# A transformer block on one core: side sums in an idle chain, Q's products and denominators reordered, result adds deferred

## The chip, the core and the metric

The kernel runs on one core of one Trainium2 chip. The core has a matmul engine (PE, TensorE), a vector engine (DVE), an activation engine (ACT), GpSimd (POOL) and a sync engine (SP) that, like POOL, issues DMAs here. The metric is the device time of one execution in microseconds (us), lower is better. A profiled execution gives a trace with every engine's instructions.

## The reference

The input x is 2048 rows of 512 in f32. A vector c gives six modulation rows through `silu(c) @ w_mod`. What is computed:

```python
h = layernorm(x) * (1 + ca) + sa
q, k, v = split(h @ wqkv)                      # 32 heads of 16
pq, pk = phi(q), phi(k)                        # phi(t) = where(t > 0, t + 1, exp(t)) + 1e-6
kv = einsum("bhsd,bhse->bhde", pk, v);  z = einsum("bhsd->bhd", pk)
o = einsum("bhqd,bhde->bhqe", pq, kv) / (einsum("bhqd,bhd->bhq", pq, z)[..., None] + 1e-6)
x = x + ga * (o @ wo)
h = layernorm(x) * (1 + cb) + sb
x = x + gb * (mish(h @ w1 + b1) @ w2)          # 512 -> 1792 -> 512
```

## The kernel before

**Tiling.** The 2048 rows are four blocks b of 512, each of four tiles t of 128 rows. Every f32 operand of a matmul is split into a rounded high part (a copy, usually on ACT) and the low part that is left (a subtraction, usually on DVE); `split` (L71) does that, with a `yield` between the two, and `mm3` (L65) multiplies with three matmuls: high x high, high x low, low x high. A unit of one 128-row tile is twelve matmuls.

**Stages, in PE's order.** For b = 1 to 3 (L726 to L775): four K units (`k_unit`), whose result goes through `phi` and `split`, then four `g_unit`s, which sum pk^T x xn over all rows into four banks gacc (so that kv = wv applied later, L930 to L944). Between them lie the transposes of the next block. In the last round come wq's splits, wo's scaling and the sums z. Then Q: for blocks 0 and 1 together by seven products instead of eight (`q_sevens` L339, one level of Strassen-Winograd, with sums of x in `q_right` and of wq in `q_left`), for blocks 2 and 3 by plain units (`q_unit`). `attend` (L778) makes the denominators on PE (den), their reciprocals on DVE, writes them to DRAM and reads them back spread over the heads (rd, by POOL's queue; for block 3 by SP's), and after `wait` more steps multiplies q with rd and splits it (qs). The matrices m = kv x wo (L954 to L957) are then used by `o_unit` (L821), which adds to the rows r. Blocks 0 to 3 are normalised again (`norm_sums` L828, `norm_each` L842, `norm_tile` L860) and transposed.

The second half, w1, Mish and w2, again uses seven products per pair of w1's columns. `rows` (L675) loads w1 and makes its sums, `columns` those of h, `product` (L1025) is one product of six matmuls (two halves c, three matmuls each). A pair is `pair_begin` (a11, a12), `pair_early` (s1, s2), `pair_middle` (s3), `pair_end` (a22, s4). Several products add up in one bank, with copies u1, u2, u3 of it taken by ACT between them; `add` (L1035) adds bank and copy on DVE, and `mish` or `later`/`mish_b` follow on ACT. `two_pairs` runs the first two pairs of a chunk interleaved. In the first chunk the gaps hold w2's product of block 0 (`d_unit`), in the last chunk (blocks 2 and 3) the units `e_unit` of a seven-product form of w2; its left operands come from `left_sums` (L1238), its right ones from `w2_sums` (L630).

**What sets the order.** The schedule is written out by hand: each engine runs its instructions in the order in which the program issues them. Beside the main line, side work is written as Python generators. `spawn` (L50) puts one into `fresh`; `tick` (L53) appends `fresh` to `running` and then takes one step of each generator in `running`, oldest first. So a tick, usually one per unit or product of PE, is what spreads side work. SBUF tiles come from one pool of 101 tiles of 512 columns (`sb`), PSUM banks from pools of 4 (acc), 3 (h) and 1 (tp); a new tile waits for the last reader of the one whose place it takes. SP and POOL issue their DMAs in order, too.

**Where the diff falls in the trace.** Early rows are `rows(0, 1)` and `rows(1, 1)` (L724). Before, the first starts with the last round's first K unit, the second is run to its end in one go after m (L958). `q_left` (L304) starts beside the g units of round 2, `q_right` (L313) beside rounds 1 and 2. In rounds 1 and 2, x's splits for tiles 2 and 3 start beside the g units of tiles 0 and 1 (L769). `W2_AT` (L628) says beside which unit of block 1's w2 stage a `w2_sums` starts; `SUMS_KEPT` names the two that stay in SBUF.

Of the kernel before, what the change touches and what calls it, by code (L numbers as in the profile page):

```python
# [13 lines left out]
P = 128  # L14
# [11 lines left out]
def block_kernel(ctx: ExitStack, tc: tile.TileContext, x, wqkv, wo, w1, b1t, w2, c, wmodt, out):  # L26
# [21 lines left out]
    running, fresh = [], []  # L48
# [195 lines left out]
    def phi(p, name, dst):  # L244

        e, r = sb(f"e_{name}"), sb(f"relu_{name}")
        act.activation(e, p, AF.Exp)  # L247
        act.activation(r, p, AF.Relu)  # L248
        yield
        dve.scalar_tensor_tensor(dst, e, 1.0, r, op0=ALU.min, op1=ALU.add)  # L250
# [89 lines left out]
    def q_sevens(side):  # L340

        pa, pc, u1, u2, u3 = {}, {}, {}, {}, {}

        def result(b, g, p, u):
            if u is not None:
                c = sb(f"cq_{b}_{g}")
                dve.tensor_tensor(c, p, u, op=ALU.add)
                p = c
            pq[b, g] = sb(f"q_{b}_{g}")
            spawn(phi(p, f"q_{b}_{g}", pq[b, g]))  # L350
# [277 lines left out]
    W2_AT = {0: 6, 1: 5, 2: 0, 3: 1, 6: 2, 10: 3, 12: 4}  # L628
# [97 lines left out]
    for b in range(1, NB):  # L726
# [3 lines left out]
        for t in range(4):  # L730
            k_unit(b, t)
            if b + 2 < NB:
                load_x(b + 2, t)
            if b == NB - 2:
                load_wqkv(0, t)
                if t == 1:
                    spawn(q_right(1))
            if last and t == 0:
                spawn(early_rows[0])
            if last:  # L740
                xn_split(b, t)
            elif t >= 2:
                xn_split(b, t - 2)
            tick()
# [4 lines left out]
        for t in range(4):  # L749
# [6 lines left out]
            if b == 1 and t == 1:  # L756
                spawn(q_right(0))
            if b == 2 and t < 2:
                spawn(q_left(t))
            if last:  # L760
                load_x(0, t, "r")
                for k in ((0, 1), (2,), (3,), ())[t]:
                    spawn(split(f"wq_{k}", wraw[0, k], wq, k))
                if t == 2:
                    z_unit()
                if t == 3:
                    spawn(z_side())
            elif t < 2:
                xn_split(b, t + 2)  # L769
# [58 lines left out]
    def norm_sums(b):  # L828

        sums = {}  # L830
        for n in range(6):
            if n < 4:
                sums[n] = act_sums("n", b, n, xt["r", b, n])
            if 0 < n < 5:
                sums_eps("n", b, n - 1, sums[n - 1])
            if n > 1:
                sums_shift("n", b, n - 2, sums[n - 2])
                v = xt["n", b, n - 2] = sb(f"n_{b}_{n - 2}")
                ln_apply("n", b, n - 2, xt["r", b, n - 2], v, act)
            yield  # L840
# [19 lines left out]
    def norm_tile(b, t):  # L860

        v = xt.pop(("r", b, t))
        if t % 2:
            ln_stats("n", b, t, v)
            ln_eps("n", b, t, t + 1)
            ln_rstd("n", b, t, t + 1)
            yield
            ln_apply("n", b, t, v, v, dve)
        else:
            sums = act_sums("n", b, t, v)  # L870
            yield
            sums_eps("n", b, t, sums)
            yield
            sums_shift("n", b, t, sums)
            ln_apply("n", b, t, v, v, act)
# [53 lines left out]
    next(early_rows[1])  # L929
# [7 lines left out]
    attending = attend(0, 4)  # L937
    next(attending)
    next(attending)
# [14 lines left out]
    for g in range(4):  # L954
        m_ps = ps("acc", f"m_ps_{g}")
        mm3(m_ps, [h[:, P * g:P * (g + 1)] for h in kvs[0]], wos[g], True, True)
        spawn(split(f"m_{g}", m_ps, ms, g))  # L957
# [80 lines left out]
    def pair_begin(c0, g, tags):  # L1038
# [3 lines left out]
        c11 = sb(f"c11_{g}")  # L1042
        add(c11, product(g, "a12", "b21", tags[1]), u1)
        return pa, c11

    def later(p, f, wait=0):
        for _ in range(wait):
            yield
        mish_b(p, f)
        yield  # L1050

    def pair_early(c0, g, pa, c11, tag):
# [5 lines left out]
        spawn(mish(c11, c0, 2 * g))  # L1060
        return pa, pc, u2

    def pair_middle(g, pa, pc, u2):
        u3, c22 = sb(f"u3_{g}"), sb(f"c22_{g}")
        product(g, "s3", "t3", onto=pa)
        act.activation(u3, pa, AF.Copy)  # L1066
        add(c22, pc, u3)
        spawn(later(c22, 2 * g + 1, 1))

    def pair_end(c0, g, pa, pc, u2, step=True):  # L1070
        c12 = sb(f"c12_{g}")
# [4 lines left out]
        add(c12, pc, u2)  # L1076
        spawn(later(c12, 2 * g, 1))
# [3 lines left out]
    def pair_unit(c0, g, odd, between):  # L1081
        begun = pair_begin(c0, g, ("tp" if odd else "h", "h"))
        tick()
        state = pair_early(c0, g, *begun, "h")
# [8 lines left out]
    def two_pairs(c0, g0, g1, begun, between):  # L1093

        s0 = pair_early(c0, g0, *begun[0], "h")
# [4 lines left out]
        pa, c11 = begun[1]  # L1100
# [3 lines left out]
        spawn(mish(c11, c0, 2 * g1))  # L1104
# [94 lines left out]
    banks, rq, U = {}, {}, {}  # L1199

# [27 lines left out]
    def left_sums(g):  # L1228
# [3 lines left out]
        dve.tensor_tensor(a22, a21, a22, op=ALU.add)  # L1232
        dve.tensor_tensor(a21, a11, a21, op=ALU.subtract)
        yield
        dve.tensor_tensor(a11, a22, a11, op=ALU.subtract)
        dve.tensor_tensor(a12, a12, a11, op=ALU.subtract)
# [4 lines left out]
    def left_trail(g):  # L1241
        yield
        yield
        yield from left_sums(g)
# [48 lines left out]
    for n, g in enumerate(pairs):  # L1293
# [97 lines left out]
```

## Time and profile before

| | |
|---|---|
| median of 3 runs | 516.07 us (515.71 to 516.18) |
| profiled execution | 515.32 us, span 513.6 us |
| PE busy | 493.6 us, 2640 matmuls, mean granted clock 0.993 |
| DVE, ACT, POOL busy | 368.9, 298.4, 144.5 us |
| HBM read, written | 62.92, 33.03 MB |

Times in the trace count from the span's start. A row of a timeline gives the start, the duration, the engine, the line, what is written and read, and in brackets the engine's idle time ahead with the instruction that ended it. A row of the waits gives who waited for whom: us in total, times, longest. A row of the windows gives the stretch, its length, the busy time of PE, of PE's weight loads, DVE, ACT and POOL with their counts, the clock granted to PE (1.00 is full), the DMA engines' mean busy share, and GB/s. Busy time of an engine is not its speed: a matmul is drawn with its whole way through the array, and the next may start before it ends.

### The profile page before, as it was taken

To read this page: it belongs to the slowest core of one execution; us is meant where nothing else is said; L and a number is where in the kernel's file an instruction comes from. 1 tells how busy PE (TensorE), PEld (TensorE's weight loads), DVE (VectorE), ACT (ScalarE), POOL (GpSimd) and SP (SyncE) were. 2 spreads that over 40 slices of the span, in tenths; PEclk is the share of its full clock that TensorE was granted. 3 is DMA by queue.
4 is the path that set the end of the run, shared out by engine and by line. 5 is a ranking of instruction groups with operands and counts; after the bars stand their busy time and mean duration, and the time that the engine had idled before them with its cause. 6 is when DMAs were issued, how large, how long until landed. Compare 5 with 4: busy or idle time off the path is not lost.

```text
span 513.6 us, 7722 instructions
## 1 busy us (share of the span) xinstructions
PE 493.6 (96%) x2640; PEld 413.5 (81%) x2640; DVE 368.9 (72%) x713; ACT 298.4 (58%) x535; POOL 144.5 (28%) x246
## 2 busy tenths in 40 slices
PE   8999997999998999998999999999998999999997
PEld 6788785878776877886788888888786888899997
DVE  6896889798979577965678763679953575549862
ACT  6868597655544498647777564358354544468200
POOL 3573020000031324111344310513454231345200
PEclk9999999999998998999999999999999999999999
DMA  8715445046844305517999956999997463497512
GB/s 298 277 39 127 123 102 144 21 133 208 260 131 123 76 18 187 199 67 265 325 340 358 333 177 210 260 373 321 378 358 219 119 185 82 125 237 214 144 42 83
DMA packets 66765, 98.58 MB, mean 192 GB/s; under 512 B 7405, under 2 KB 31861, under 8 KB 66726
## 3 DMA queue, kind: packets, MB, share of 16 engines
q0 software_dynamic: 29360, 45.31, 32.3%
q1 hardware_dynamic: 37220, 52.51, 30.6%
q8 instruction: 21, 0.34, 0.3%
q10 hardware_dynamic: 146, 0.26, 0.1%
q14 instruction: 18, 0.15, 0.1%
HBM read 62.92 MB, written 33.03 MB: 187 GB/s over the span
## 4 chain that ended last, share of the span: by engine, by line
PE 71%; DVE 11%; ACT 8%; issue 5%; DMA 3%; POOL 0%; ACTq 0%; POOLq 0%; DVEq 0%
PE p_a L1031 17%; PE p_s L1031 7%; PE oacc L69 5%; PE oacc L67 5%; PE oacc L68 5%; PE m L69 5%; PE m L68 5%; PE m L67 5%; PE o L67 2%; PE o L69 2%; PE o L68 2%; PE gacc L69 2%; PE gacc L68 2%; ACT x L201 1%; PE gacc L67 1%
## 5 line engine op out<-in xcount | busy, mean ns | idle before, releaser
L1036 DVE TENSOR_TENSOR c<-p_s,u 128x512 f32<-128x512 f32 x28 | 19.3, 691 | 72.0 <-ACT u L1066 61.5
L1059 ACT ACTIVATE u<-p_a 128x512 f32<-128x512 f32 x12 | 7.2, 598 | 30.6 <-PE p_a L1031 30.6
L1023 ACT ACTIVATE ub<-c,b1c 128x512 f32<-128x512 f32 x28 | 20.0, 717 | 3.7 <-DVE c L1036 3.5
L1291 POOL DMA_DIRECT2D wt_m<-w2t x20 | 14.0, 702 | 26.0 <-PE m L69 17.2
L891 ACT ACTIVATE hf_n<-tp_n,mc 128x512 f32<-128x512 f32 x16 | 11.7, 771 | 15.7 <-PE tp_n L889 15.7
L192 POOL TENSOR_TENSOR rs_n<-rs_n,half 128x1 f32<-128x1 f32 x16 | 10.0, 626 | 30.5 <-DVE rs_n L187 14.5
L790 POOL DMA_DIRECT2D rden_d<-rden x3 | 2.2, 717 | 54.0 <-DVE rden L788 54.0
L1041 ACT ACTIVATE u<-p_a 128x512 f32<-128x512 f32 x14 | 8.3, 594 | 15.0 <-PE p_a L1031 15.0
L247 ACT ACTIVATE e_k<-pk 128x512 f32<-128x512 f32 x16 | 9.5, 594 | 11.9 <-PE pk L69 11.9
L1066 ACT ACTIVATE u<-p_a 128x512 f32<-128x512 f32 x14 | 8.3, 594 | 13.0 <-PE p_a L1031 13.0
L673 POOL DMA_DIRECT2D w2b<-w2d x20 | 10.6, 552 | 18.1 <-issue 5.6
L250 DVE SCALAR_TENSOR_TENSOR ku<-e_k,relu_k 128x512 f32<-128x512 f32 x16 | 11.0, 689 | 6.4 <-ACT relu_k L248 6.4
L814 DVE TENSOR_TENSOR r<-o,r 128x512 f32<-128x512 f32 x16 | 11.0, 686 | 6.4 <-PE o L69 6.4
L1036 DVE TENSOR_TENSOR c<-p_a,u 128x512 f32<-128x512 f32 x14 | 9.6, 689 | 7.2 <-PE p_a L1031 5.0
L250 DVE SCALAR_TENSOR_TENSOR q<-e_q,relu_q 128x512 f32<-128x512 f32 x16 | 10.8, 689 | 5.1 <-ACT relu_q L248 5.1
L201 ACT ACTIVATE x<-x,nb_x,rs_x 128x512 f32<-128x512 f32 x15 | 11.4, 809 | 5.3 <-DVE nb_x L196 4.9
L192 POOL TENSOR_TENSOR rs_x<-rs_x,half 128x1 f32<-128x1 f32 (+1 forms) x10 | 7.4, 742 | 24.2 <-DVE rs_x L187 23.4
L1000 ACT ACTIVATE u<-p_a,b1c 128x512 f32<-128x512 f32 x14 | 9.5, 680 | 7.2 <-PE p_a L1031 7.2
L667 POOL DMA_DIRECT2D wb<-w2d x14 | 9.9, 709 | 12.7 <-ACT u L1000 8.4
L259 POOL DMA_DIRECT2D ku<-ku x8 | 7.1, 893 | 18.6 <-DVE ku L250 17.9
L878 POOL DMA_DIRECT2D nd<-r x8 | 4.5, 565 | 26.7 <-ACT r L201 26.7
L802 DVE SCALAR_TENSOR_TENSOR q<-q,rd 128x512 f32<-128x512 f32 x16 | 10.4, 690 | 1.7 <-DMA rd<-rden_d 1.7
(1569 smaller groups left out, 1986.1 us busy)
## 6 DMA issues: line engine op xcount, KB each, us to landing
wm<-in_wmodt_dram SPq DMA_DIRECT2D x24, 256.0 KB, 2.8
w2b<-w2d POOLq DMA_DIRECT2D x20, 256.0 KB, 6.2
wt_m<-w2t POOLq DMA_DIRECT2D x20, 256.0 KB, 3.6
r<-in_x_dram SPq DMA_DIRECT2D x16, 256.0 KB, 3.2
x<-in_x_dram SPq DMA_DIRECT2D x15, 256.0 KB, 4.8
w1p<-in_w_dram SPq DMA_DIRECT2D x14, 256.0 KB, 3.6
w2r<-in_w_dram SPq DMA_DIRECT2D x14, 256.0 KB, 3.5
wb<-w2d POOLq DMA_DIRECT2D x14, 256.0 KB, 4.4
```

Source lines behind the costliest of these rows:

```text
L67: pe.matmul(o, st[0], mv[0], start=start, stop=False)
L68: pe.matmul(o, st[0], mv[1], start=False, stop=False)
L69: pe.matmul(o, st[1], mv[0], start=False, stop=stop)
L192: pool.tensor_tensor(y, y, half[:, lo:hi], op=ALU.pow)
L201: act.activation(dst, t, AF.Identity, bias=nb[key, b][:, j:j + 1], scale=rs[key, b][:, j:j + 1])
L250: dve.scalar_tensor_tensor(dst, e, 1.0, r, op0=ALU.min, op1=ALU.add)
L814: dve.tensor_tensor(r, p, r, op=ALU.add)
L891: act.activation(hf[b, j], p, AF.Identity, bias=mc[:, 12 + j:13 + j], scale=mc[:, 16 + j:17 + j])
L1023: act.activation(u, p, AF.Mish, bias=b1c[:, f:f + 1])
L1031: pe.matmul(p, st, mv, start=onto is None and c == 0 and i == 0, stop=c == 1 and i == 2, skip_group_check=onto is not None)
L1036: dve.tensor_tensor(out, p, u, op=ALU.add)
L1291: pool.dma_start(v, w2t[g][:, :, SUM[name], :])
```

## The change

A second list of generators, `idle_work`, is stepped at the end of each tick, only its first two (three in the last chunk). Into it go Q's right and left sums, the early rows, the left sums of the last chunk and the two kept w2 sums; several of them start later than before. Splits of x in rounds 1 and 2 start beside the K units, as in round 3. In `q_sevens`, s1 comes after a22, and phi of a sum waits one tick. den(0) comes after the first Q unit of block 2, den(1) after the third, with m's products between. Block 0's norm starts tile by tile. The adds of the pairs' results become generators of their own, issued in the tick behind. One `norm_next` goes, `norm_tile` yields once more, and the order of the first units in the last chunk's gaps changes.

The diff, cut to its core:

```diff
+    def spawn_idle(gen):
+        idle_work.append(gen)
     def tick():
...
+        for g in idle_work[:width[0]]:          # width is [2], in the last chunk [3]
+            if next(g, "end") == "end":
+                idle_work.remove(g)
...
-    def phi(p, name, dst):
+    def phi(p, name, dst, wait=False):
+        if wait:
+            yield
...
         for o in range(2):                       # in q_sevens
-            pc[o] = q_product(o, "s1", "t1", ("h", "acc")[o])
             q_product(o, "s3", "t3", onto=pa[o])
             u3[o] = copy(pa[o], f"qu3_{o}")
-            result(1, 2 + o, pc[o], u3[o])
-            side(3 + o)
+        side(3)
         for o in range(2):
             result(0, 2 + o, q_product(o, "a22", "t4", onto=pa[o]), None)
+        side(4)
+        for o in range(2):
+            pc[o] = q_product(o, "s1", "t1", ("h", "acc")[o])
+            result(1, 2 + o, pc[o], u3[o])
         side(5)
...
-    W2_AT = {0: 6, 1: 5, 2: 0, 3: 1, 6: 2, 10: 3, 12: 4}
+    W2_AT = {0: 6, 1: 5, 2: 0, 3: 1, 6: 2}
...
                 if t == 1:                       # K units of rounds 1 to 3
-                    spawn(q_right(1))
-            if last and t == 0:
-                spawn(early_rows[0])
-            if last:
-                xn_split(b, t)
-            elif t >= 2:
-                xn_split(b, t - 2)
+                    spawn_idle(q_right(1))
+            if last and t < 2:
+                spawn_idle(q_left(t))
+            if last and t == 2:
+                spawn_idle(early_rows[0])
+            xn_split(b, t)
...
             if b == 1 and t == 1:                # g units
-                spawn(q_right(0))
-            if b == 2 and t < 2:
-                spawn(q_left(t))
+                spawn_idle(q_right(0))
...
-            elif t < 2:
-                xn_split(b, t + 2)
...
-    def norm_sums(b):
...
+    def norm_first(t):                           # one step each: nothing, sums, eps, shift, apply
...
             sums_shift("n", b, t, sums)          # norm_tile
+            yield
             ln_apply("n", b, t, v, v, act)
...
-    next(early_rows[1])
...
-    attending = attend(0, 4)                     # after kv's product
-    next(attending)
-    next(attending)
...
-    spawn(attending)
+    attending = attend(0, 3)
     for g in range(4):
         q_unit(2, g)
+        if g == 0:
+            next(attending)
+            next(attending)
         if g == 1:
+            spawn(attending)
+        if g == 2:
             spawn(attend(1, 4))
+        if g == 1:
             spawn(mod_side(range(12, 16), 1))
         load_x(3, g, "r")
+        if g == 2:
+            for k in range(4):                   # m's products, from behind this loop
...
         tick()
-    run(early_rows[1])
     for g in range(4):
         q_unit(3, g)
         tick()
         if g == 1:
             for t in range(4):
                 o_unit(0, t)
+                spawn(norm_first(t))
...
-            spawn(norm_sums(0))
+            spawn_idle(early_rows[1])
...
-        c11 = sb(f"c11_{g}")                     # pair_begin
-        add(c11, product(g, "a12", "b21", tags[1]), u1)
-        return pa, c11
+        c11, p = sb(f"c11_{g}"), product(g, "a12", "b21", tags[1])
+        def result():
+            add(c11, p, u1)
+            yield
+            yield from mish(c11, c0, 2 * g)
+        spawn(result())
+        return pa
+    def result_b(p, u, f):
+        c = sb(f"cb_{f}")
+        add(c, p, u)
+        yield
+        mish_b(c, f)
...
-        add(c22, pc, u3)                         # pair_middle
-        spawn(later(c22, 2 * g + 1, 1))
+        spawn(result_b(pc, u3, 2 * g + 1))
...
-        add(c12, pc, u2)                         # pair_end
-        spawn(later(c12, 2 * g, 1))
+        spawn(result_b(pc, u2, 2 * g))
...
-            norm_next()                          # first chunk, g == 1, ahead of two_pairs
...
+        for n, (d, u, v, op) in enumerate(...):  # left_sums: a step for each sum if fine
+            if fine or n == 2:
+                yield
+            dve.tensor_tensor(d, u, v, op=op)
...
+        if n in (3, 5):                          # last chunk
+            spawn_idle(w2_sums(SUMS_KEPT[n // 2 - 1]))
...
-            two_pairs(L, pairs[0], g, begun, (gap(0, 0), gap(1, 0)))
+            two_pairs(L, pairs[0], g, begun, (gap(0, 0), gap(0, 1)))
             for i in range(2):
-                spawn(left_trail(pairs[i]))
+                spawn_idle(left_trail(pairs[i]))
         else:
-            pair_unit(L, g, n % 2, (gap(0, n - 1), gap(1, n - 1)))
+            pair_unit(L, g, n % 2, (gap(1, 0), gap(1, 1)) if n == 2 else (gap(0, n - 1), gap(1, n - 1)))
             if n < EARLY:
-                spawn(left_trail(g))
+                spawn_idle(left_trail(g))
```

More of the change, by code (lines that the diff above doesn't have):

```diff
@@ L349, in result @@
             pq[b, g] = sb(f"q_{b}_{g}")
-            spawn(phi(p, f"q_{b}_{g}", pq[b, g]))
+            spawn(phi(p, f"q_{b}_{g}", pq[b, g], u is not None))
         def copy(p, name):
@@ L826, in o_unit @@
         spawn(o_post(p, b, t))
-    def norm_sums(b):
[L830 to L840, printed above, removed]
+    def norm_first(t):
+        yield
+        sums = act_sums("n", 0, t, xt["r", 0, t])
+        yield
+        sums_eps("n", 0, t, sums)
+        yield
+        sums_shift("n", 0, t, sums)
+        yield
+        v = xt["n", 0, t] = sb(f"n_0_{t}")
+        ln_apply("n", 0, t, xt["r", 0, t], v, act)
     def norm_each(b, t):
@@ L1041, in pair_begin, with pair_early @@
         act.activation(u1, pa, AF.Copy)
-        c11 = sb(f"c11_{g}")
-        add(c11, product(g, "a12", "b21", tags[1]), u1)
-        return pa, c11
-    def later(p, f, wait=0):
-        for _ in range(wait):
-            yield
-        mish_b(p, f)
+        c11, p = sb(f"c11_{g}"), product(g, "a12", "b21", tags[1])
+        def result():
+            add(c11, p, u1)
+            yield
+            yield from mish(c11, c0, 2 * g)
[4 more added lines that the diff above has]
+        add(c, p, u)
         yield
-    def pair_early(c0, g, pa, c11, tag):
+        mish_b(c, f)
+    def pair_early(g, pa, tag):
         u2 = sb(f"u2_{g}")
@@ L1199, in block_kernel @@
     banks, rq, U = {}, {}, {}
+    width[0] = 3
     def load_r(n, c):
@@ L1226, in e_unit, with left_sums @@
         seventh(("m1", "m2")[c], "acc", ag[L, 2 * g + c], [w[:, c, :] for w in wb[g]], n, G - 1)
-    def left_sums(g):
+    def left_sums(g, fine=False):
         a11, a12, a21, a22 = ua[2 * g], ua[2 * g + 1], ub[2 * g], ub[2 * g + 1]
         yield from split(f"l4_{g}", a22, left, ("m4", g))
[L1232 to L1236, printed above, removed]
+        for n, (d, u, v, op) in enumerate(((a22, a21, a22, ALU.add), (a21, a11, a21, ALU.subtract),
+                                           (a11, a22, a11, ALU.subtract), (a12, a12, a11, ALU.subtract))):
+            if fine or n == 2:
+                yield
+            dve.tensor_tensor(d, u, v, op=op)
         sums_of[g] = {"m5": a22, "m7": a21, "m6": a11, "m3": a12}
@@ L1243, in left_trail @@
         yield
-        yield from left_sums(g)
+        yield from left_sums(g, True)
     def left_prep(name, g):
```

21 lines of the change are left out of this document (9 added, 12 removed).

## The prediction

> **What bounds the kernel now.** I read the page's busy shares and its chain first, then the waits of TensorE (PE), then the windows of each stage with their clock.
>
> ```profile
> PE 493.6 (96%) x2640; PEld 413.5 (81%) x2640; DVE 368.9 (72%) x713; ACT 298.4 (58%) x535; POOL 144.5 (28%) x246
> ...
> PE 71%; DVE 11%; ACT 8%; issue 5%; DMA 3%; POOL 0%; ACTq 0%; POOLq 0%; DVEq 0%
> ```
>
> PE is busy for 493.6 of 513.6 us, and the change takes no matmul away. So all that can be won is what PE loses: its gaps, and stretches at a lower clock. The gaps by what ended them, from the waits of PE (us in total, times, longest):
>
> ```profile
> PE m L69 <- DVE a_11l L81: 2.4, 1, 2.4
> PE tp_n L889 <- ACT n L201: 2.2, 1, 2.2
> PE o L67 <- DVE m_0l L81: 1.9, 1, 1.9
> PE gacc L69 <- DVE xn_2l L81: 1.9, 1, 1.9
> PE gacc L69 <- DVE xn_3l L81: 1.8, 2, 0.9
> PE p_a L1031 <- ACT u L1066: 1.5, 1, 1.5
> ...
> PE den L783 <- DVE q L250: 0.8, 2, 0.7
> ...
> PE den L783 <- ACT gb_row L390: 0.4, 1, 0.4
> PE p_s L1031 <- DVE c L1036: 0.3, 1, 0.3
> ```
>
> These sum to 13.2 us; every one of them lies in code that the diff touches. The rest of PE's idle time is the start (before 36 us) and the tail, which the diff leaves alone. A gap costs a little more than its row, as two neighbouring matmuls of a dense stretch show:
>
> ```profile
> 36.63 0.39 PE L67 MATMUL pk<-wk_0h,hT_x_0h 128*128 128x512 f32 x1
> 36.86 0.39 PE L68 MATMUL pk<-wk_0l,hT_x_0h 128*128 128x512 f32 x1
> ```
>
> A matmul is drawn 0.39 long but the next starts 0.23 after it, so a gap costs its row plus 0.16. Twelve matmuls, one unit of a 128-row tile, take 2.72 us. Now the clock (the column behind POOL), in four stretches, each just behind a gap:
>
> ```profile
> 83.40:86.80 3.40, 2.96 (x12) 2.12 (x12) 3.37 (x9) 3.11 (x6) 0.00 (x0) 1.00 0.28 104
> ...
> 160.00:163.40 3.40, 3.40 (x9) 2.60 (x9) 3.40 (x7) 1.25 (x4) 0.00 (x0) 0.51 0.15 35
> ...
> 194.50:198.00 3.50, 3.50 (x11) 2.80 (x10) 1.68 (x6) 3.50 (x7) 0.93 (x1) 0.55 0.51 191
> ...
> 390.50:394.00 3.50, 3.48 (x20) 3.11 (x21) 0.00 (x0) 0.59 (x1) 0.56 (x2) 1.00 0.08 16
> ```
>
> Behind the gaps of m_0l and n the clock was about half for 3.4 us: 3.4 x 0.49 = 1.7 and 3.5 x 0.45 = 1.6 us lost. Behind the 1.9 of xn_2l and the 2.4 of a_11l it stayed full. I count the 3.3 us as caused by those two gaps. [...]
>
> **The change part by part.** DVE and ACT work through their instructions in program order, so putting work "behind all else" in a tick only moves it behind that tick's other work; the next tick's work still stands behind it.
>
> *Rounds b = 1, 2: splits of x earlier, Q's left sums out.* The late xn_2l of round 2, on DVE:
>
> ```profile
> 79.32 0.42 DVE L305 TENSOR_TENSOR qs<-wr,wr 128x256 f32<-128x256 f32 x1
> ...
> 80.78 0.68 DVE L168 SCALAR_TENSOR_TENSOR wm<-wm,sc_row 128x512 f32<-128x512 f32 x1
> ...
> 82.00 0.69 DVE L83 SCALAR_TENSOR_TENSOR pk_3l<-ku,pk_3h 128x512 fp32r<-128x512 f32 x1
> 82.60 0.68 DVE L81 TENSOR_TENSOR xn_2l<-x,xn_2h 128x512 fp32r<-128x512 f32 x1
> ...
> 93.67 0.69 DVE L250 SCALAR_TENSOR_TENSOR ku<-e_k,relu_k 128x512 f32<-128x512 f32 x1 [2.88 <-ACT relu_k L248]
> ```
>
> A 128x512 instruction costs DVE 0.60 from start to start, four 128x256 sums 1.46. Each q_left holds 1.46 + 2 x 0.60 = 2.7 us of DVE and two ACT copies. Both leave the stage in which DVE is full, and go to the K units of the last round, where DVE now stands idle for 2.88 us and the early rows (4.2 us: four sums, three and a half low parts) have gone one stage on. xn_2l and xn_3l are issued two ticks earlier, about 5 us, against gaps of 0.9 to 1.9. Next late there is pk_3l: its ku, pk_3h and low part come at about 81.8 in the old clock less the stages' gain, 0.3 before PE asks. So the 3.7 us of xn gaps go, with 3 x 0.16 = 4.2. What comes back, on ACT:
>
> ```profile
> 46.13 0.64 ACT L75 ACTIVATE xn_0h<-x 128x512 fp32r<-128x512 f32 x1
> 46.65 1.52 ACT L201 ACTIVATE x<-x,nb_x,rs_x 128x512 f32<-128x512 f32 x2
> ```
>
> In round 1 two more of these copies (0.52 each) stand ahead of the applies of x; one of them falls on time that ACT waits for PE, and the transposes that wait for the second pair come 0.5 later. Net **-3.7**.
>
> *Early rows 0 one stage later.* Their two w1 loads now stand on SP's queue behind the first load of r, which takes a tile that the first g unit frees; they land before the sums are due two ticks on, or the sums hold DVE back. The nearest thing that PE waits for there is z:
>
> ```profile
> 107.98 0.69 DVE L257 TENSOR_TENSOR ku<-ku,ku 128x512 f32<-128x512 f32 x1
> ...
> 108.91 1.06 PE L286 MATMUL z<-ku,ones 128*32 128x512 f32 x8
> ```
>
> The add comes 0.2 before z now; with the sums behind it, and PE 3.7 earlier, I work out 0.9 before. Cost 0; if the loads came a tick late, up to 2.7.
>
> *Q's products.* s1 moves behind a22. Every copy of a bank (0.60 on ACT) must be done within one product (1.36) before PE adds to the bank again; phi now yields once, so that ACT doesn't stand waiting for DVE's add ahead of these copies. The first add is due on DVE behind z_side's 4.7 us and the last two low parts of the early rows; I find a22 ready 0.5 before PE asks. Cost 0, from 0 to 1.
>
> *Denominators, kv, m.* One Q unit (2.72) now stands between q's last sums and den(0), and den(1) comes behind m: the den gaps go (0.8 + 0.4), **-1.2**. kv's low part has 0.2 in hand before the m products. The early rows' burst that stood ahead of m_0l goes:
>
> ```profile
> 149.50 0.42 DVE L686 TENSOR_TENSOR s<-w1p 128x256 f32<-128x256 f32 x1
> ...
> 153.53 0.69 DVE L81 TENSOR_TENSOR qs_0l<-q,qs_0h 128x512 fp32r<-128x512 f32 x1
> ...
> 158.96 0.69 DVE L81 TENSOR_TENSOR m_0l<-m_ps,m_0h 128x512 fp32r<-128x512 f32 x1
> ```
>
> That is 4.0 us from DVE, and the m parts move two ticks up: the 1.9 of m_0l goes, with 0.16 and the clock's 1.7: -3.8. But den(0) later means the reciprocals come back later:
>
> ```profile
> 136.82 0.35 DVE L787 TENSOR_SCALAR rden<-den,tiny_den 128x128 f32<-128x128 f32 x1 [0.55 <-PE den L783]
> ...
> 146.43 0.69 DVE L802 SCALAR_TENSOR_TENSOR q<-q,rd 128x512 f32<-128x512 f32 x1 [0.54 <-DMA rd<-rden_d]
> 148.29 0.69 DVE L802 SCALAR_TENSOR_TENSOR q<-q,rd 128x512 f32<-128x512 f32 x1 [1.17 <-DMA rd<-rden_d]
> ...
> 167.00 1.08 PE L783 MATMUL den<-q,hmask 128*32 128x128 f32 x32
> ```
>
> From rden to the second product with rd are 11.5 us, through two DMAs. From the end K of kv's product: one unit 2.7, den 1.0, 0.2 to DVE, so rden at K + 3.9, the second product at K + 15.4 to 16.0. Queued behind it on DVE: a sum of q, rden(1) with its reciprocal (1.3), four m low parts, two of qs, two products, a column, a sum of q, then qs_2l: 11 x 0.60 + 1.3 + 0.6 = 8.5, at K + 24.5. PE reaches o(0,0) after six Q units, two den, m and a transpose at K + 21.3 and asks for qs_2l 1.8 later, at K + 23.1. A new wait of **1.4**, bounds 0 (rd a little sooner) and 3.1 (1.4 and a half clock, 1.7, as behind the 1.9). Net **-2.4**.
>
> *norm_first and early rows 1.* Sums, shift and apply of block 0 start three ticks earlier, the last tile's two, where ACT is nearly idle; the rows' 4.0 us of DVE come behind, spread over five ticks. n is then ready about a unit before its transposes, so the 2.2 goes with 0.16 and the clock's 1.6: **-3.9**. Next late is qs_2l of block 2, behind those rows: 0.4 in hand.
>
> *Pairs, first chunk.* ACT's copy u (L1066) stood behind an apply that waited for DVE:
>
> ```profile
> 237.01 0.82 ACT L201 ACTIVATE r<-r,nb_n,rs_n 128x512 f32<-128x512 f32 x1 [3.31 <-DVE nb_n L222]
> ...
> 245.47 0.67 ACT L1000 ACTIVATE u<-p_a,b1c 128x512 f32<-128x512 f32 x1
> ...
> 246.70 0.68 DVE L1036 TENSOR_TENSOR c<-p_s,u 128x512 f32<-128x512 f32 x1
> ```
>
> That norm_next goes and norm_tile yields before its apply: the 1.5 and 0.16 go. The other gap, 0.3 + 0.16, is the add c that frees the bank for the next s1. It is now issued behind the low part of the last half, which waits for the Mish of 245.47 and its copy, and the norm's ACT sums (1.5) now stand just ahead of that Mish: about 1.0 in place of 0.46. In later pairs I find the add 0.7 before PE asks. Net 2.1 - 1.0 = **-1.1**.
>
> *Pairs, last chunk.* DVE's a_11l stood behind an add that waited for ACT:
>
> ```profile
> 388.57 0.69 DVE L1036 TENSOR_TENSOR c<-p_s,u 128x512 f32<-128x512 f32 x1 [2.76 <-ACT u L1066]
> ```
>
> The add now comes last in its tick, and the unit in the gap uses a_12 instead of a_11, ready a product earlier: **-2.5**. The left sums one at a time and two w2 sums (2.6 us of DVE each, their w2p loads on SP, four copies on ACT) come into pairs 2 to 6, where DVE has about a third of its time free; second() loses the same, where PE never waits. Cost 0 as long as the loads are there (rival three).
>
> Sum: 3.7 + 1.2 + 2.4 + 3.9 + 1.1 + 2.5 = 14.8. The profiled execution took 515.32 (span 513.6 and 1.7 around it): 500.5. It is 0.75 below the median 516.07, so in terms of the median **501.3**.
>
> **The rivals.**
>
> *One: the waits come back.* PE runs ahead of DVE and ACT by what it no longer loses, and margins of 0.2 to 0.9 (kv's low part, a22's copy, z, pk_3l, qs_2l twice) give. Half of six such margins missing by 1 us each, 3, and half a clock behind two of them, 3.3: 501.3 + 6.3 = 507.6. For it: DVE is full in most of these stages. Against it: the removed loads are larger than the delays.
>
> *Two: the slow stretches aren't the gaps'.* If they stay, 501.3 + 3.3 = 504.6. Against it: both follow a gap at once; for it: two equal gaps had none. [...]
>
> *Three: slower.* In the last chunk the w2 sums stand on DVE two ticks behind their own loads, and DVE can't pass them. From the instructions of the w2p loads, and SP's waits between 370 and 480 us:
>
> ```profile
> DMA to landing us min/median/max: 9.1/9.2/9.6
> ...
> SPq L1205 <- DMA wb<-w2d: 18.9, 1, 18.9
> ```
>
> Two ticks are 5.4 us, and the next add c has 2.7 before PE wants its bank: beyond 8.1 us from issue every microsecond stalls PE. Landing alone, 9.2, costs 1.1 twice. If the loads wait for a free tile as rq's did, 18.9, each costs 10.8: 501.3 + 21.6 = 522.9. Against it: SP stood ahead of PE there, so its wait cost nothing, and the 9.2 are from a stage with DMAs busier than this one.
>
> *Four: it doesn't do what it says.* The chain still stands ahead of the next tick, other work is late by the same amount, the gaps change their names: 514 to 517.
>
> **How the numbers follow.** Forecast 0.60 (498.5 to 504.5), rival two 0.05, one 0.20 (504.5 to 510), four 0.05, three 0.10. The lowest is all gaps gone with nothing back: 13.2 + 10 x 0.16 + 3.3 = 18.1, so 498.0. The range from 498 to 510 leaves out rivals three and four and the edges of the others. A measurement of this kernel tells about 0.2% (1 us) from no change: faster 0.87, same 0.03, slower 0.10.
>
> **What would show it.** Right: no PE wait on xn_2l, xn_3l, m_0l, n, L1066 or a_11l; DVE between 79 and 90 without L305 to L308; clock 1.00 in all windows after 36 us; at o(0,0) one wait on qs_2l of about 1.4, at the third pair's s1 one on c of about 1.0. Wrong: PE gaps on z, kvl, u of Q, or DVE waiting on w2p or w1p loads. The prediction fails most easily if one of the new orders stops DVE on a load, since everything else queues behind it.

## The result, and the profile after

The changed kernel took 502.37 us (median of 4 executions, 501.10 to 503.08), against 515.89 for the kernel before, measured beside it (515.13 to 516.18): a ratio of 0.9737, interval 0.9712 to 0.9763. The forecast was 501.3, with a range from 498 to 510. In a later series the same kernel took 502.91 beside 515.34, ratio 0.9762 (0.9739 to 0.9785).

The profiled execution took 501.73, its span is 499.9. The page's busy shares and its chain:

```profile
PE 489.5 (98%) x2640; PEld 411.1 (82%) x2640; DVE 367.9 (74%) x713; ACT 298.7 (60%) x535; POOL 145.2 (29%) x246
...
PE 80%; DVE 10%; ACT 4%; DMA 3%; issue 1%; POOL 1%; POOLq 0%; DVEq 0%; ACTq 0%
```

PE is now on the chain for 80% of the span (71% before). Who makes it wait, beside its start, is in the waits of PE:

```profile
PE o L76 <- DVE qs_2l L88: 1.0, 1, 1.0
PE p_s L1039 <- DVE nb_n L229: 0.8, 1, 0.8
PE o L74 <- ACT qs_2h L82: 0.7, 1, 0.7
PE tp_x L474 <- ACT x L208: 0.7, 2, 0.4
PE pq_s L345 <- DVE cq L356: 0.7, 1, 0.7
...
PE tp_n L894 <- ACT n L208: 0.2, 1, 0.2
```

Of the nine rows that the prediction lists seven are gone (xn_2l, xn_3l, both of den, m_0l, u, a_11l) and n has 0.2 of 2.2. The ninth, the add ahead of the third pair's s1, grew from 0.3 to 0.8, as forecast; the view puts it down to nb_n, the instruction that VectorE did next. New and forecast is the wait at the first o unit, on qs_2h and qs_2l. New and not forecast is the one on cq. The windows by stage (length, PE busy, then the others, the clock behind POOL):

```profile
90.00:135.00 45.00, 44.31 (x279) 34.97 (x278) 41.58 (x93) 30.32 (x57) 1.17 (x2) 1.00 0.56 170
135.00:160.00 25.00, 23.25 (x127) 17.89 (x126) 19.70 (x39) 9.82 (x19) 7.38 (x12) 1.00 0.50 123
160.00:200.00 40.00, 39.67 (x241) 31.96 (x240) 34.43 (x77) 33.18 (x65) 13.10 (x21) 1.00 0.45 135
200.00:250.00 50.00, 49.22 (x219) 40.40 (x219) 40.00 (x75) 34.00 (x63) 10.58 (x20) 1.00 0.71 241
250.00:385.00 135.00, 135.00 (x623) 112.09 (x622) 86.58 (x163) 75.00 (x133) 53.41 (x97) 1.00 0.96 301
385.00:446.00 61.00, 61.00 (x338) 53.13 (x337) 36.75 (x62) 33.49 (x55) 17.56 (x27) 1.00 0.59 155
```

The clock is 1.00 in all of them: both stretches of half clock are gone, and the mean clock was 1.00 in all four executions. From 250 to 446 PE is never idle, though two more sums of w2 are made there. The idle time that is left in these rows is 1.75 us in 135:160, at the first o unit, 0.69 ahead of it, 0.33 behind it and 0.78 in 200:250, at the third pair's s1.

### The profile page after: what moved, and what is told of

Same layout as the page of the kernel before. It is cut to its first block, busy times and chain, and to the rows that moved or that the text cites. A ratio compares the mean times of both kernels' runs of the same rounds, so it can differ in the third digit from the quotient of the medians.

```text
span 499.9 us, 7705 instructions
## 1 busy us (share of the span) xinstructions
PE 489.5 (98%) x2640; PEld 411.1 (82%) x2640; DVE 367.9 (74%) x713; ACT 298.7 (60%) x535; POOL 145.2 (29%) x246
## 4 chain that ended last, share of the span: by engine, by line
PE 80%; DVE 10%; ACT 4%; DMA 3%; issue 1%; POOL 1%; POOLq 0%; DVEq 0%; ACTq 0%
PE p_a L1039 18%; PE p_s L1039 7%; PE oacc L76 5%; PE oacc L75 5%; PE oacc L74 5%; PE m L76 5%; PE m L75 5%; PE m L74 5%; PE gacc L75 3%; PE gacc L76 3%; PE gacc L74 3%; PE pk L76 2%; PE pk L74 2%; PE pk L75 2%; PE pq_a L345 2%; DMA rden_d<-rden 1%
## 5 line engine op out<-in xcount | busy, mean ns | idle before, releaser
L1044 DVE TENSOR_TENSOR cb<-p_s,u 128x512 f32<-128x512 f32 x28 | 19.2, 686 | 12.1 <-ACT u L1080 12.1
L1031 ACT ACTIVATE ub<-cb,b1c 128x512 f32<-128x512 f32 x28 | 20.0, 717 | 5.7 <-DVE cb L1044 5.6
L896 ACT ACTIVATE hf_n<-tp_n,mc 128x512 f32<-128x512 f32 x16 | 11.7, 769 | 12.8 <-PE tp_n L894 12.8
L208 ACT ACTIVATE x<-x,nb_x,rs_x 128x512 f32<-128x512 f32 x15 | 11.5, 809 | 4.3 <-DVE nb_x L203 3.8
L731 POOL DMA_DIRECT2D a1b<-rd_a x10 | 5.4, 541 | 19.8 <-PE p_a L1039 8.1
L190 DVE BATCH_NORM_STATS2 st_x<-x 128x6 f32<-128x512 f32 x13 | 8.9, 682 | 3.0 <-DMA x<-in_x_dram 3.0
```

The lines of the kernel that those rows point to most:

```text
L208: act.activation(dst, t, AF.Identity, bias=nb[key, b][:, j:j + 1], scale=rs[key, b][:, j:j + 1])
L896: act.activation(hf[b, j], p, AF.Identity, bias=mc[:, 12 + j:13 + j], scale=mc[:, 16 + j:17 + j])
L1031: act.activation(u, p, AF.Mish, bias=b1c[:, f:f + 1])
L1044: dve.tensor_tensor(out, p, u, op=ALU.add)
```

## The experiments

All ratios below are to the kernel before, measured in the same series; each edit is made in the changed kernel. There were three series behind that of the result, so kernels are compared by their ratios and by the gaps in their traces.

| kernel | us | ratio (interval) |
|---|---|---|
| changed, first series | 502.37 | 0.9737 (0.9712 to 0.9763) |
| changed, again (after_again) | 502.91 | 0.9762 (0.9739 to 0.9785) |
| u_xn | 505.07 | 0.9815 (0.9788 to 0.9841) |
| u_norm | 508.76 | 0.9888 (0.9862 to 0.9915) |
| u_gap | 502.66 | 0.9761 (0.9739 to 0.9782) |
| u_adds | 502.24 | 0.9759 (0.9731 to 0.9787) |
| u_gap_adds | 504.59 | 0.9784 (0.9745 to 0.9822) |
| u_normnext | 504.07 | 0.9790 (0.9757 to 0.9823) |
| u_rows | 503.72 | 0.9775 (0.9738 to 0.9811) |
| i_o | 504.83 | 0.9798 (0.9776 to 0.9821) |
| u_den | 498.42 | 0.9672 (0.9652 to 0.9691) |
| i_best | 498.69 | 0.9674 (0.9653 to 0.9695) |
| i_best2 | 500.27 | 0.9716 (0.9689 to 0.9742) |

The theory was that each wait has an edit of its own, and that the two stretches of half clock hang on the gaps ahead of them. The rivals: the clock goes its own way; other parts of the change removed the waits.

**Splits of xn (u_xn).**

```diff
-            xn_split(b, t)
+            if last: xn_split(b, t)
+            elif t >= 2: xn_split(b, t - 2)          # K units
...
+            if not last and t < 2: xn_split(b, t + 2)  # g units
```

> The changed kernel with one part undone: in rounds 1 and 2 the halves of xn are again made by units 2 and 3 of k and units 0 and 1 of g. Theory (each gap of TensorE has its own edit): the gaps of stretch 36:90 come back, 4.06 us idle against 0.52 + 0.3 now, so 3.3 to 4.2 us longer than the changed kernel, 505.7 to 506.6 us, with waits on xn in the records at their old places. Rival (the sums for Q, moved into the idle work, had filled those units, and the order of xn matters little): under 1.0 us longer, 502.4 to 503.4.

Two gaps came back in the timeline of PE:

```profile
73.71 0.50 PE L76 MATMUL gacc<-pk_0h,xn_0l 128*128 128x512 f32 x1 [0.87 <-DVE xn_0l L88]
81.59 0.50 PE L76 MATMUL gacc<-pk_2h,xn_2l 128*128 128x512 f32 x1 [0.95 <-DVE xn_2l L88]
```

That is 1.8 us, z starts 2.2 later (106.00 against 103.80), and the ratio is 0.5 to 0.8% up. So the earlier splits are worth about half of the 4.06 us that PE idled in that stage before. By what is left, the other half went with the work that left the stage (the sums for Q), which this kernel still keeps out of it; that was not tried alone. Neither expectation came true as a whole: the size lies between the two, and only xn_2l's wait is at an old place. The two on xn_3l stayed away, and the one on xn_0l is new.

**Norm of block 0, and the clock (u_norm).**

```diff
-                spawn(norm_first(t))
...
+            spawn(norm_sums(0))      # behind the four o units
```

> The changed kernel with block 0's norm again made by one loop over its four tiles behind all four o units. Theory: the wait of the first transpose of n, 0.20 us now and 2.22 before, comes back, and so does the stretch of half clock behind it (0.91 over 160:200 before), together 3.4 to 4.0 us, 505.8 to 506.4 us. [...]

Its span is 507.2, 7.3 us longer, more than the 3.4 to 4.0 expected. The wait for n came back larger than it was before, since PE comes to block 0's transposes 4.5 us earlier (186.61 against 191.14) and the n that it waits for last only 2.5 earlier (191.30 against 193.85):

```profile
PE tp_n L908 <- ACT n L208: 4.0, 2, 3.3
```

And the clock fell twice. The stretches begin at 157.98 and 192.11 and last 3.41 us each; these are the 3.41 us ahead of them and the stretches themselves:

```profile
154.57:157.98 3.41, 1.73 (x7) 1.15 (x7) 3.41 (x7) 3.12 (x6) 1.73 (x3) 1.00 0.71 181
157.98:161.39 3.41, 3.41 (x9) 2.65 (x9) 3.41 (x10) 0.00 (x0) 0.00 (x0) 0.50 1.11 202
...
188.70:192.11 3.41, 0.81 (x6) 0.80 (x7) 3.34 (x11) 2.10 (x5) 1.04 (x2) 1.00 0.23 83
192.11:195.52 3.41, 3.41 (x9) 2.64 (x8) 1.53 (x6) 3.41 (x6) 0.92 (x1) 0.50 0.51 181
```

With the gap of n there is a stretch of half clock behind it, without it there is none: the rival that the clock goes its own way falls. (In i_o below, a gap of 2.5 at n is followed by one too, from 188.0.) The other stretch follows three small gaps at the first o unit (0.61, 0.72, 0.96), none of which would have been suspected alone. That place lies ahead of the edit, so this stretch is not the edit's own; yet all four executions of u_norm lost the clock of two stretches or more (mean clock 0.989 to 0.992), and why is open. Gaps, 3.8 (4.0 against 0.2), and two stretches of half clock, 3.4, make 7.2; without the first stretch the edit's own price is 5.5. What the traces show of the clock stands at the end.

**The last chunk's a_11l: order of the gaps, or the place of the adds (u_gap, u_adds, u_gap_adds).**

```diff
-            two_pairs(L, pairs[0], g, begun, (gap(0, 0), gap(0, 1)))      # u_gap, u_gap_adds
+            two_pairs(L, pairs[0], g, begun, (gap(0, 0), gap(1, 0)))
-            pair_unit(L, g, n % 2, (gap(1, 0), gap(1, 1)) if n == 2 else ...)
+            pair_unit(L, g, n % 2, (gap(0, n - 1), gap(1, n - 1)))
...
-        spawn(result_b(pc, u3, 2 * g + 1))        # u_adds, u_gap_adds; likewise c11 and c12
+        c = sb(f"cb_{2 * g + 1}"); add(c, pc, u3)
+        spawn(result_b(c, 2 * g + 1))             # only Mish left to the next tick
```

> The changed kernel with the order of the work between the halves of the last chunk's first pairs undone: (0,0), (1,0) between the first two, then (0,1), (1,1). Theory: e(1,0) again asks for a_11l before VectorE has made it, a wait of 2.2 to 2.6 us near the start of the last chunk's pairs, 504.6 to 505.0 us. Rival (the results' later place on VectorE is what removed that wait): under 0.6 us longer, 502.4 to 503.0.

> The changed kernel with the sums for c11, c22 and c12 issued again at once, ahead of the halves due, and only Mish left to the next tick; the order of the gaps stays as changed. Theory: the waits of the first chunk's first pairs come back (2.1 us before), the wait of 0.8 us at the third pair's s1 goes; 1.0 to 1.6 us longer, 503.4 to 504.0 us; a_11l is not waited for. Rival (the later place is what removed the wait for a_11l): that wait of 2.5 us is there as well, 505.9 to 506.5 us. Second rival (it does nothing for TensorE in either chunk): 501.4 to 502.4.

> The changed kernel with both the results' adds issued at once and the old order of the gaps in the last chunk; each alone brought no wait for a_11l. Theory (either of the two is enough by itself): with both undone the wait for a_11l of 2.2 to 2.6 us is back, 2.4 us longer than with one undone (near 504.5), and a stretch of half clock, 1.7 us, may follow it. Rival (a third part removed it: the left sums out of that stage): no wait for a_11l, as long as the changed kernel within 0.7 us.

Neither edit alone brought a wait for a_11l; both together did. The wait of PE and, from VectorE's timeline, its cause:

```profile
PE m L76 <- DVE a_11l L88: 1.8, 1, 1.8
```

```profile
378.06 0.69 DVE L1044 TENSOR_TENSOR cb<-p_s,u 128x512 f32<-128x512 f32 x1 [2.76 <-ACT u L1079]
378.67 0.68 DVE L88 TENSOR_TENSOR a_11l<-u,a_11h 128x512 fp32r<-128x512 f32 x1
```

That is the picture of before, to the 2.76 us: an add that waits for ScalarE's copy stands ahead of a_11l. So each of the two parts removes this wait by itself, and the change makes both. The times alone would not tell: u_gap_adds' interval overlaps those of u_gap and u_adds, and its half clock (157.4 to 160.8 in the trace) lies at the first o unit, which neither edit touches. The theory of u_gap, that the order of the gaps removed the wait, and the rival of u_adds, that the later adds did, are both wrong as they stand. In u_adds the wait at the third pair's s1 went, as its theory had it, but the first pairs' waits that the theory wanted back did not come: PE is busy for 50.00 of 50 us from 200 to 250 there. In that stage the later adds cost 0.8 us and, with the norm out, bring nothing.

**The norm ahead of the first pairs (u_normnext).**

```diff
+            norm_next()              # first chunk, g == 1, ahead of two_pairs
...
-            yield                    # norm_tile, ahead of its apply
```

> The changed kernel with the norm of one more tile again begun ahead of the first two pairs, and its apply again without a tick of its own. Theory (this norm alone made the first chunk's waits, not the place of the adds): ScalarE stands before an apply again, and the 1.5 us wait for u or one like it comes back between 200 and 250, 1.0 to 1.7 us longer. Rival (the place of the adds removed them): under 0.4 us longer, no new wait there.

```profile
PE p_s L1038 <- DVE cb L1043: 1.5, 1, 1.5
```

The wait at the third pair's s1 grew from 0.8 to 1.5. ScalarE stands before an apply again (2.18 us, 3.31 before), but the 1.5 us wait for u did not come back: PE idles 1.54 from 200 to 250 here, 0.78 in the changed kernel, none in u_adds and 1.79 in the kernel before. So leaving this norm out, with a tick for its apply, is enough by itself to remove the wait for u (u_adds), and with the later adds that wait stays away even when the norm is back. Whether both undone together bring it back, as with a_11l, was not run. (The kernel's 504.07 holds one or two stretches of half clock as well, in each of its four executions (mean clock 0.993 to 0.997); in the trace they lie at the first o unit, from 157.10 to 163.92, which the edit doesn't touch.)

**The burst of early rows (u_rows).**

```diff
+    next(early_rows[1])              # ahead of kv's product
...
+    run(early_rows[1])               # ahead of the last Q block
-            spawn_idle(early_rows[1])
```

> The changed kernel with the second early rows of w1 again made in one burst ahead of the last Q block (sums and low parts, 4.0 us of VectorE, which now stand right ahead of qs_0l). Theory: qs_0l, now ready as TensorE asks, comes 4.0 us late, so the first o unit loses 4.0 us more than now, and a window of half clock, 1.7 us, follows: 4.0 to 6.0 us longer than the changed kernel, with the wait named qs_0l. Rival (VectorE has this time free, it waits 4.35 us for rd just before): under 1.0 us longer.

```profile
PE o L76 <- DVE qs_0l L88: 2.9, 1, 2.9
```

The wait is where the theory put it: the burst stands on VectorE from 151.35 to 154.95, right ahead of qs_0l. It is 2.9 us and the other two of that unit shrank to 1.2, so the unit idled 4.1 against 1.7, 2.4 more, not 4.0: in this execution rd's second product came 0.8 sooner (146.55 against 147.32), and the later waits were in part absorbed by the first. That is one execution, and the slowest. The wait for qs_0l was from none (u_gap) to 1.5 us (u_normnext) in kernels whose edits don't touch that stage. By the medians the burst costs 0.7 to 2 us, and the interval overlaps the changed kernel's; the four executions had from none to two stretches of half clock (mean clock 1.00 to 0.993), and the one without (502.06) took no longer than the changed kernel's 502.19 and 502.47. So its price in time is not shown.

**The place of den(0) (u_den), and of the first o unit (i_o).**

```diff
-        if g == 0:                   # u_den: den(0) back ahead of q_unit(2, 0)
-            next(attending)
-            next(attending)
+    attending = attend(0, 3)
+    next(attending)
+    next(attending)
...
-        if g == 1:                   # i_o: block 0's o units behind q_unit(3, 2)
+        if g == 2:
             for t in range(4):
                 o_unit(0, t)
...
-                if t == 1:           # i_o, too: den(2) starts one o unit sooner
+                if t == 0:
                     spawn(attend(2, 5))
```

> The changed kernel with den(0) again ahead of the first unit of Q's block 2. Theory (what the prediction gave as the price of its later place): the den gap of 0.8 to 1.2 us is back, and the reciprocals come 2.7 us sooner, so the 2.0 us of waits at the first o unit go: 0.8 to 1.2 us shorter than the changed kernel. Rival (there VectorE's own queue, not the reciprocals, makes qs_2l late): the den gap is back and the waits stay, 0.8 to 1.2 us longer.

> The changed kernel with one edit: block 0's o units stand behind the third unit of the last Q block in place of the second. Theory: the two waits on qs_2h and qs_2l (0.73 and 0.96, 2.0 us from start to start) go, and with them any half clock there; the n transposes lose up to 0.6; 1.4 to 2.2 us shorter than the changed kernel. Rival (n or the next qs come later by as much): within 0.5 us of it.

u_den is 4.5 us faster than the changed kernel in its own series (0.9672 against 0.9762, intervals apart), and neither expectation had that: the waits at the first o unit went, as the theory said, but the den gap did not come back. In its timeline, den follows kv's product at once, with no bracket behind it:

```profile
128.35 2.08 PE L940 MATMUL kv_ps<-zs,wv 128*64 128x64 f32 x64
130.36 1.08 PE L789 MATMUL den<-q,hmask 128*32 128x128 f32 x32
```

Its windows beside the two of the changed kernel above:

```profile
135.00:160.00 25.00, 25.00 (x166) 20.00 (x165) 22.11 (x42) 13.01 (x27) 6.64 (x11) 1.00 0.71 157
160.00:200.00 40.00, 39.97 (x219) 32.81 (x218) 33.85 (x74) 34.13 (x64) 13.75 (x23) 1.00 0.38 119
```

No idle time is left at the first o unit. PE starts z at the same time in both kernels, 103.8, and ends 3.5 us earlier in u_den (the last rows of PE's timelines, the changed kernel first):

```profile
496.24 0.28 PE L76 MATMUL m<-wt_m,l_m_4l 128*128 128x256 f32 x1
```

```profile
492.77 0.28 PE L76 MATMUL m<-wt_m,l_m_4l 128*128 128x256 f32 x1
```

Of these 3.5, 2.6 come at the first o unit (from start to start) and 0.4 at n. Part of what is left of the 4.5 is half clock: two of the changed kernel's four executions in that series had one stretch of it (mean clock 0.997), u_den's none (0.999 or more). i_o shows the other side. Moving the o units cleared all but 0.7 of their waits but cost 1.1 at block 3's den and 2.5 at n:

```profile
PE tp_n L894 <- ACT n L208: 2.5, 1, 2.5
PE den L789 <- DVE q L259: 1.1, 1, 1.1
```

with half clock in every execution (mean clock 0.995 to 0.997); it is 1.9 us slower than the changed kernel, though the intervals overlap. The rival named the right place, n, but not the size: it had the two within 0.5 us.

**The changed kernel again (after_again).** No edit.

> The changed kernel as it is, beside the others of this call. [...] Rival (the clock follows the single gap, and none of its gaps is above 1.2): clock 1.00 in all executions.

Two executions at clock 1.00 (502.19, 502.47), two at 0.997 (503.35, 504.10). One stretch of 3.41 us at half clock is 1.7 / 502 = 0.0034 of the mean clock, so these two had one. With the four of the first series, six of eight had none. The rival falls; why two executions had a stretch and six did not is not shown.

**Three edits against the three waits (i_best, i_best2).**

```diff
-        if n == 1:
             spawn(kv_side())
+        if n == 2:                   # i_best and i_best2; with u_adds' and i_o's edits
             spawn(mod_side([20, 21, 22, 23, 16, 17, 18, 19], 2))
...
-        if g == 2:                   # i_best2: m's products one Q unit later
+        if g == 3:
             for k in range(4):
                 m_ps = ps("acc", f"m_ps_{k}")
```

> The changed kernel with three more edits against its three new waits: the eight columns of w_mod one tick later (cq's add ahead of them, 0.84 us of gap at s4 now), block 0's o units behind the third unit of the last Q block in place of the second (2.0 us of gaps now), and the adds at once (0.94 us now at the third pair's s1). Theory: these waits go and no other comes, 3.0 to 3.8 us shorter than the changed kernel. Rival (the o units one place later make n or the next qs late by as much): 0.5 to 1.8 us shorter, with a wait for n or for qs of block 1 near 2 us.

> The version with the three edits of i_best, and m's products one unit of Q later, behind the last one of block 2: their wait for kvl (0.9 us) was new there. Theory: that wait goes, m_0l still comes before the o units, which stand one unit later too: 0.7 to 1.1 us shorter than i_best, ratio to before near 0.966. Rival (m's low parts then stand ahead of qs_0l on VectorE and make it late): as long as i_best or up to 1 us longer, with a wait on qs at the first o unit.

i_best is 0.6% faster than the changed kernel was in the first series and 0.9% than in the last, 3.2 to 4.5 us, near the theory's 3.0 to 3.8. The three waits are gone, but others came, which the theory had ruled out: m waits 0.9 for kvl, n takes 0.6 (0.2 in the changed kernel) and a den 0.4. i_best2 took the wait for kvl away and got a larger one at n (2.0 us). It is 1.6 us slower, 2.2 by the ratios, with intervals that overlap: more than its rival's 1 us, and at another place. i_best and u_den beat both kernels. They mend the first o unit from two sides; u_den with i_best's columns and adds was not run.

## Why the prediction was right, and where it was not

**The bound.** Right: PE's gaps and the clock behind two of them were what there was to win. From 36 to 446 us PE's idle time fell from 13.5 to 4.1, and with the 3.4 of half clock that is 12.8 of the 13.7 by which the span fell; what a gap costs beyond its row (below) has room for the rest. The sum was 14.8, the profiled executions differ by 13.6. That the two are so close is in part luck, as the terms missed in both directions. The starts of the same matmuls in the two traces show it:

| stage, up to | before | after | gained | forecast |
|---|---|---|---|---|
| rounds 1 to 3, to z | 108.91 | 103.80 | 5.1 | 3.7 |
| Q's products, to kv's product | 132.40 | 128.37 | -1.1 | 0 |
| den and m, to the first transpose of n | 191.14 | 184.46 | 2.7 | 1.2 + 2.4 |
| n, to the first chunk | 215.23 | 205.33 | 3.2 | 3.9 |
| first chunk, to the last | 369.96 | 358.64 | 1.4 | 1.1 |
| last chunk, to the last matmul | 509.92 | 496.24 | 2.4 | 2.5 |

What a gap costs beyond its row was sized too small. I took a gap's row plus 0.16, but the matmul behind a gap is drawn longer and the next one comes 0.34 after it, not 0.23, so a gap between such matmuls costs its row plus 0.27. The first o unit of the changed kernel shows it:

```profile
154.78 0.50 PE L74 MATMUL o<-m_2h,qs_2h 128*128 128x512 f32 x1 [0.73 <-ACT qs_2h L82]
155.12 0.40 PE L75 MATMUL o<-m_2l,qs_2h 128*128 128x512 f32 x1
156.48 0.50 PE L76 MATMUL o<-m_2h,qs_2l 128*128 128x512 f32 x1 [0.96 <-DVE qs_2l L88]
156.81 0.39 PE L74 MATMUL o<-m_3h,qs_3h 128*128 128x512 f32 x1
```

The rows that the prediction sums also hold eleven gaps; its lowest time counts ten.

**Rounds 1 and 2, -3.7.** Right in kind, and rather more: z starts 5.1 earlier, of which 0.2 is there at the first K unit already (36.41 against 36.63). The 0.5 at tp_x is there: from the first transposes to the next g unit it takes 1.75, and took 1.22. u_xn splits the gain between the two edits.

**Q's products, cost 0.** This step failed. I looked at ScalarE's copies of the first bank, which are done in time, and not at the second bank: s4 adds onto pc, which VectorE's add for cq must have read first. s1 now comes right ahead of s4, and two columns of w_mod and a sum of q stand ahead of that add:

```profile
122.86 0.69 DVE L175 SCALAR_TENSOR_TENSOR wm<-wm,sc_row 128x512 f32<-128x512 f32 x1
...
124.09 0.69 DVE L259 SCALAR_TENSOR_TENSOR q<-e_q,relu_q 128x512 f32<-128x512 f32 x1
124.69 1.28 DVE L356 TENSOR_TENSOR cq<-pq_s,qu 128x512 f32<-128x512 f32 x2
```

The price is 0.69 and the 0.27 on top of it, near 1, the upper end of the 0 to 1 that I had kept. i_best, with the columns a tick later, has no such wait.

**Den, -1.2.** The gap went, for another reason than the one given. I credited the Q unit now between q's sums and den(0). u_den has no such unit and no gap. That Q's last product for block 0, a22, now comes two products sooner is what fits; it was not tried alone. So the move of den(0) bought nothing and cost what it delayed.

**m, -2.4.** m_0l's wait and its half clock went as stated, and the new wait came at the unit stated: 0.73 on qs_2h and 0.96 on qs_2l for a forecast of 1.4, and the unit took 5.32 from start to start (152.18 to 157.50) in place of 2.72. It is larger because the time from rden to the second product with rd was 12.84 (134.48 to 147.32), not 11.5:

```profile
134.48 0.35 DVE L793 TENSOR_SCALAR rden<-den,tiny_den 128x128 f32<-128x128 f32 x1 [2.90 <-PE den L789]
...
147.32 0.69 DVE L808 SCALAR_TENSOR_TENSOR q<-q,rd 128x512 f32<-128x512 f32 x1 [0.89 <-DMA rd<-rden_d]
```

I had seen that the later den(0) causes this wait, and did not ask whether den(0) had to be later.

**n, -3.9.** Right in kind: 0.2 of 2.2 is left, and the half clock went with it. u_norm brings both back together. The stage as a whole gained 3.2 of the 3.9; where the rest went was not traced.

**First pairs, -1.1.** Right in size (0.78 for a forecast of 1.0 at the third pair's s1, no wait for u), and right that the later adds cause the wait at s1 (u_adds). That the norm caused the wait for u is half shown: without the norm the wait is gone, but with the norm alone back (u_normnext) it didn't return.

**Last chunk, -2.5.** Right: no a_11l, no wait from 250 on. I had named both edits as one cause; each is enough.

**The rivals.** Waits did come back (rival one), but as one missed margin and two forecast ones, not six. The clock (rival two): with the gaps at m_0l and n gone it was 1.00 in all four executions, and with n's gap back half clock came back behind it (u_norm). Rival three, the w2 loads: from 385 to 446 PE has no idle time. Rival four, the same waits under other names: 13.5 us faster leaves no room for it.

## What to carry to other kernels

When a wait for a late result is to go, first try the order of what makes the result, and look at the wait again before the consumer is moved: den(0) behind a Q unit delayed two DMAs and VectorE's queue behind them, and 3.5 us of PE hung on the end. For every bank that a product adds to, list who must have read it and what stands ahead of that reader in its engine's queue, for the second bank as for the first. Undo parts of a composite change in pairs where each alone shows nothing; at a_11l one of two edits was spare, and in the first chunk the pair that would tell was not run.

## What the runs showed of the hardware

**Half clock came in stretches of 3.41 us.** Every stretch of half clock in these traces is 3.41 us long, or 6.83 (u_rows, u_normnext). In the kernel before they start at 160.08 and 194.21, in u_norm at 157.98 and 192.11. PE's busy time in the kernel before, in the 3.41 us ahead of each stretch, in the stretches themselves, and at two gaps behind which the clock stayed full (xn_2l's, the first row, and u's, the last):

```profile
81.57:84.98 3.41, 1.64 (x7) 1.38 (x8) 3.38 (x8) 3.35 (x7) 0.00 (x0) 1.00 0.50 158
156.67:160.08 3.41, 1.51 (x8) 0.93 (x7) 3.41 (x7) 3.41 (x9) 0.38 (x1) 1.00 1.01 247
160.08:163.49 3.41, 3.41 (x10) 2.63 (x9) 3.41 (x7) 1.26 (x4) 0.00 (x0) 0.50 0.12 29
190.80:194.21 3.41, 1.19 (x9) 0.82 (x8) 3.31 (x11) 2.18 (x6) 1.48 (x2) 1.00 0.09 24
194.21:197.62 3.41, 3.41 (x11) 2.79 (x10) 1.94 (x7) 3.41 (x6) 0.93 (x1) 0.50 0.49 184
238.59:242.00 3.41, 1.92 (x9) 1.30 (x8) 0.53 (x1) 3.35 (x7) 0.12 (x1) 1.00 1.04 387
```

Ahead of half clock PE had 1.51 and 1.19 us of work in 3.41 here, 1.73 and 0.81 in u_norm, 1.73 in u_gap_adds, 1.64 in u_normnext and 1.19 in u_rows. That alone does not tell: in the kernel before, the 3.41 us from 387.36 to 390.77, with the gap of a_11l, hold 1.03 of work, and the clock is 1.00 there and behind it. The length of a gap does not tell either: the 1.90 at m_0l and the 2.22 at n were followed by half clock, the 1.89 at xn_2l and the 2.38 at a_11l were not. Three gaps of 0.6 to 1.0 were followed by it in u_norm, and nearly the same three (0.67, 0.74, 0.96) were not in u_adds. In these traces half clock stands only behind gaps; why it follows some and not others they do not show. Left open, too: all 23 executions of the kernel before in the three series lost at least the clock of two stretches (mean clock 0.989 to 0.993; two stretches of 3.41 make 0.993).

**The same DMAs took longer.** The four loads of rd for the first block took a median of 4.8 us from issue to landing in the kernel before and 6.4 in the changed one (issues of 118 to 150 us):

```profile
rd<-rden_d POOLq DMA_DIRECT2D x4, 256.0 KB, 4.8
```

```profile
rd<-rden_d POOLq DMA_DIRECT2D x4, 256.0 KB, 6.4
```

In i_o, whose code is that of the changed kernel up to there, it was 7.4. In u_den it was 4.5 (of five loads) and in i_best, where w_mod's columns come a tick later, 4.6. So the loads that the first o unit waits for varied between two executions of the same code, 6.4 and 7.4. Which other transfers make the difference was not tried.
